# A table for the full-array work between attention visits: two linear attention layers and two segment-memory layers on one Trainium2 core

## The chip, the cores and the metric

The kernel runs on one core of one Trainium2 chip. The metric is device time in microseconds for one execution; lower is better. Before the change the median of three runs is 1875.67 us (1871.93 to 1879.55).

## The reference

The input x has 2048 tokens of 512 features in float32. Four layers follow each other, A, B, A, B, each on the layer norm of x and each added to x. The weights of the two A layers are the same, and those of the two B layers too. There are 32 heads of 16 features.

```python
# A: linear attention with a learned feature map
phi_q = concat([softmax(pq), softmax(-pq)])          # pq = q @ w_phi per head
phi_k = concat([softmax(pk), softmax(-pk)])
kv, z = phi_k^T v, sum(phi_k)
o = (phi_q kv) / (phi_q z + 1e-6);  x = x + o @ wo

# B: four segments of 512 tokens, causal softmax inside, a memory across
for s in range(4):
    logits = qs @ ks^T * scale + mask;  a_dot = softmax(logits) @ vs
    pq = elu1(qs);  a_mem = (pq M) / (pq z + 1e-6)
    o = g * a_mem + (1 - g) * a_dot                   # g = sigmoid(beta) per head
    pk = elu1(ks);  M = M + pk^T vs;  z = z + sum(pk)
x = x + o @ wo
```

Here elu1(t) is t + 1 for positive t and exp(t) otherwise.

## The kernel before, in words

**Precision and shapes.** Every large product of the projections is split into a high and a low float32r part, and three products (high-high, high-low, low-high) for each of four blocks of 128 input features are summed. So one result tile of 128 x 512 is a *group of twelve products* of 128x128 by 128x512 (`mm3`, L304). Its result stands in a PSUM tile with the tag `g`; there are three of these (`G = 3`). The attention products have tiles of their own, one each: `lg` for logits, `mx` for maxima, `pv` for values.

**Layer A** (L431) has two passes. Pass 1 takes keys and values of all tokens into one state; its queries go to DRAM. Pass 2 (L544) takes the 16 token tiles of 128 in turn: eight transposes of the features, eight products with the state KN, four transposes of the result (`turn`, L319) and one group of twelve for the output projection. A tile uses a `g` tile six times.

**Layer B** (L580) runs in steps k (L874). One *visit* is 4 heads of one segment of 512 tokens, 8 visits to a segment and 32 in all, and five steps to a visit (`R = 5`). In each step from k = 0 to 159 TensorE first multiplies logits (`attend`, L751), from which ScalarE makes the exponential P, and GpSimd masks it. From k = -9 it multiplies the logits of a later visit once more for their maxima (`maxima`, L710), which VectorE reduces to one number a row. In steps 0 and 2 of a visit the values follow (`weighted`, L787). Steps 1, 3 and 4 (`FILL`, L32) have a *gap* instead: full-array work of other parts. A visit further needs `put_maxima` (L742, one transpose and a copy back into the queries) and `finish` (L814, four transposes of the attention result U and, on VectorE, a reciprocal and a product `wt`, in `weigh`, L343).

**What fills the gaps.** For each segment: the layer norm of its tokens and their transposes (`norm_T`, L257); eight query and key projections (`proj`, L633), four values (`values`, L607) and four output projections of the segment before (`out`, L822), 16 groups of twelve; the memory's reads, transposes and update (`memory`, L658). From k = -31 to about 1 the rest of pass 2 of the layer A before runs in the same steps, from its token tile 7 on. In the last segment of the first layer B the norm and the values of the next layer A's first segment come along.

**What sets the order.** TensorE's instructions are chained in the order in which the code issues them while the steps run (`held`, L107). From k = 3 VectorE, ScalarE and GpSimd are chained likewise (`Ordered`, L89). A planner decides what stands in a gap. `plan` (L840) gives each job its slots and a cost; at each slot it issues products one by one until the job's due share is done. `rest` (L863) holds values and output projections, which are issued, also one by one, until the gap has the work that `FULL` names. So a projection is stretched over eight to ten steps, a values or output group often over several gaps, and while it is open it keeps its `g` tile. The call at the centre is:

```python
while rest and k >= rest[0][1] and (work[0] - begun + own < full[max(k - R, 0) // (8 * R)]
                                    or k >= rest[0][2]):
```

**Other steps that the change touches.** `queue_w` (L625) issues the DMA for the weights of a later projection; two weight tiles `w4` are in flight. `stack` (L699) copies the parts of a projection by six DMAs into the row layout of the attention products, at step 0 of a visit, three visits ahead of its logits. `phi` (L616) makes the feature map of a projection in the step after it: two activations on ScalarE, two operations on GpSimd. `residual` (L331) loads the tile of x to which an output projection is added. All these DMAs are issued by SyncE's queue.

Of the kernel before, what the change touches and what calls it, by code (L numbers as in the profile page):

```python
# [18 lines left out]
P = 128  # L19
NSEG = 4  # L20
# [26 lines left out]
SIDE = 1.0  # L47
# [4 lines left out]
def interleave_kernel(ctx, tc, x_in, a_wqkv, a_wphi, a_wo, b_wq, b_wk, b_wv, b_wo, b_beta,  # L52
# [251 lines left out]
    def mm3(po, lhs, rhs, fine=False):  # L304

        n = 0
        for kc in range(NC):
            for a, b in ((0, 0), (0, 1), (1, 0)):
                mm(po, lhsT=lhs(a, kc), rhs=rhs(b, kc), start=(n == 0), stop=(n == 11))
                n += 1  # L310
                if fine and n < 12:
                    yield
            if not fine:
                yield

    def tok_proj(po, hT, t, w, fine=False):
        yield from mm3(po, lambda a, kc: hT[a][:, kc, t * P : (t + 1) * P], lambda b, kc: w[b][:, kc, :], fine)
# [19 lines left out]
    def out_proj(x, xdst, i, o, w, fine=False):  # L337
        po = PS("g", G)
        yield from mm3(po, lambda a, kc: o[a][:, kc * P : (kc + 1) * P], lambda b, kc: w[b][:, kc, :], fine)
# [20 lines left out]
    def v_tile(hT, w, vv, tag, fine=False):  # L360
# [4 lines left out]
        for t in range(4):  # L365
            po = PS(*tag)
            yield from tok_proj(po, hT, t, w, fine)
            act.copy(v[:, t, 0 : H * VW].rearrange("p (h e) -> p h e", e=VW)[:, :, 0:DH],
                           po.rearrange("p (h e) -> p h e", e=DH))

# [60 lines left out]
    class LayerA:  # L431
# [4 lines left out]
        def pass1(self, first):  # L436
            hTs, vv = [], []
            norm = norm_T(self.xsrc, 0, hTs)
# [141 lines left out]
    class LayerB:  # L580
# [21 lines left out]
        def turned(self, s):  # L602

            for _ in self.ng:
                yield

        def values(self, s):  # L607
            self.vv[s] = []
            yield from v_tile(self.hT[s], self.wv, self.vv[s], ("g", G), True)
            self.valued = s  # L610
# [4 lines left out]

        def phi(self, d, m, pp):  # L616
            e = T2("tb2", TB2)
            r = T2("tb3", 2)
            act.activation(e, pp, AF.Exp)
            act.activation(r, pp, AF.Relu)  # L620
            pool.tensor_scalar(e, e, 1.0, None, op0=MIN)
            pool.tensor_tensor(out=e, in0=e, in1=r, op=ADD)
            d["phi", m] = e
# [9 lines left out]
        def proj(self, s, c):  # L633
            d = self.st[s, c] = {}
            hT = self.hT[s]
            need = (s > 0, s < NSEG - 1)
            for m in range(2):
                w = self.w4.pop(0)
                pp = PS("g", G)
                yield from mm3(pp, lambda a, kc: w[:, a, kc, :], lambda b, kc: hT[b][:, kc, :], True)  # L640
                self.queue_w()
                hi, lo = d["part", m] = [self.part() for _ in range(2)]
                act.copy(hi, pp)
                dve.tensor_tensor(out=lo, in0=pp, in1=hi.bitcast(F32), op=SUB)
# [4 lines left out]
            self.ready.add(s * NC + c)  # L649
# [8 lines left out]
        def memory(self, s, c):  # L658
# [14 lines left out]
            if s < NSEG - 1:  # L673
# [7 lines left out]
                assert self.valued >= s  # L681
# [140 lines left out]
        def out(self, s):  # L822
# [4 lines left out]
            for t in range(4):  # L827
                cur, xc = oT, x
                if t < 3:
# [3 lines left out]
                yield from out_proj(xc, self.xdst, 4 * s + t, cur, self.wo, True)  # L833
# [6 lines left out]
        def plan(self, extra):  # L840


            S = 8 * R

            def span(a, b):
                return [k for k in range(a, b) if self.filled(k)]

            yield from extra
            yield self.turned(0), span(-30, -26), 0
# [21 lines left out]
        def filled(self, k):  # L871
            return k < -LEAD or k % R in FILL
# [145 lines left out]
```

## Time and profile before

| what | value |
|---|---|
| median of three runs | 1875.67 us (1871.93 to 1879.55) |
| the profiled execution's own time | 1861.92 us |
| its span, first to last instruction | 1860.2 us |
| mean granted TensorE clock | 0.950 |
| busy: TensorE, its weight loads | 1584.2 us (85%), 1116.3 us (60%) |
| busy: VectorE, ScalarE, GpSimd | 1182.7 us (64%), 789.8 us (42%), 542.3 us (29%) |
| chain of work that ended last | TensorE 60%, VectorE 23%, ScalarE 6%, DMA 4% |

In the profile PE is TensorE, PEld its weight loads, DVE VectorE, ACT ScalarE, POOL GpSimd, SP SyncE. A row names the result tile and its inputs: `g<-w,hh` is a product of the values projection, `g<-w,oh` of an output projection, `g<-hh,wqk` of a query or key projection, `g<-ident,U` a transpose of U. L119 is the line of every product and L123 that of every transpose, since both go through a helper; L98 is the line of every instruction of the other three engines that the ordering class issues. In square brackets or behind the bar stands how long the engine was idle before an instruction, and what ended that. A group of products that waits for a buffer is put down to whoever read that buffer last. The page's times are of one execution.

### The profile page before, as it was taken

To read this page: it belongs to the slowest core of one execution; us is meant where nothing else is said; L and a number is where in the kernel's file an instruction comes from. 1 tells how busy PE (TensorE), PEld (TensorE's weight loads), DVE (VectorE), ACT (ScalarE), POOL (GpSimd) and SP (SyncE) were. 2 spreads that over 40 slices of the span, in tenths; PEclk is the share of its full clock that TensorE was granted. 3 is DMA by queue.
4 is the path that set the end of the run, shared out by engine and by line. 5 is a ranking of instruction groups with operands and counts; after the bars stand their busy time and mean duration, and the time that the engine had idled before them with its cause. 6 is when DMAs were issued, how large, how long until landed. Compare 5 with 4: busy or idle time off the path is not lost.

```text
span 1860.2 us, 28201 instructions
## 1 busy us (share of the span) xinstructions
PE 1584.2 (85%) x9856; PEld 1116.3 (60%) x9856; DVE 1182.7 (64%) x3358; ACT 789.8 (42%) x1202; POOL 542.3 (29%) x840
## 2 busy tenths in 40 slices
PE   5999897778888888897999998877888888888987
PEld 4888775544555555554568887665455555555544
DVE  4676773367777567567736676625767766665783
ACT  6443242125555345355533333311365544453543
POOL 3322320113433334232230233210234423332322
PEclk9999898899999999998999998988999999999999
DMA  9512343323444333234422035322433233333321
GB/s 317 190 55 88 92 135 136 91 75 102 126 119 116 86 78 105 81 108 148 132 94 76 23 93 169 102 85 80 131 105 95 75 100 89 92 80 83 97 68 46
DMA packets 99974, 193.68 MB, mean 104 GB/s; under 512 B 13432, under 2 KB 27000, under 8 KB 96760
## 3 DMA queue, kind: packets, MB, share of 16 engines
q1 hardware_dynamic: 98680, 191.35, 34.4%
q8 instruction: 79, 1.29, 0.3%
q10 hardware_dynamic: 1152, 0.52, 0.1%
q14 instruction: 63, 0.52, 0.1%
HBM read 96.86 MB, written 41.94 MB: 75 GB/s over the span
## 4 chain that ended last, share of the span: by engine, by line
PE 60%; DVE 23%; ACT 6%; DMA 4%; issue 4%; SPq 1%; POOL 1%; POOLq 0%; DVEq 0%; ACTq 0%
PE g L119 38%; DVE mx L98 12%; PE mx L119 7%; PE lg L119 6%; PE g L123 5%; PE pv L119 4%; ACT P L98 2%; DVE mxs L98 2%; DMA x<-x 1%; DVE es L98 1%; ACT ta L98 1%; ACT x L98 1%; DMA tb<-pq 1%; DVE ta L98 1%; DVE r L98 1%
## 5 line engine op out<-in xcount | busy, mean ns | idle before, releaser
L98 DVE CUSTOM_DVE_ANT_0 mx<-mx,mask 128x128 f32<-128x128 f32 (+3 forms) x1024 | 510.2, 498 | 238.0 <-PE mx L119 213.8
L98 ACT ACTIVATE P<-lg 128x1024 f32<-128x1024 f32 x320 | 328.1, 1025 | 319.2 <-PE lg L119 310.2
L98 POOL TENSOR_SCALAR_AFFINE_SELECT P<-P 128x256 f32<-128x256 f32 (+1 forms) x448 | 190.6, 439 | 638.8 <-ACT P L98 638.7
L119 PE MATMUL mx<-e,e 63*128 63x256 f32 (+2 forms) x1024 | 155.2, 361 | 60.0 <-DVE mxs L98 52.4
L119 PE MATMUL g<-w,oh 128*128 128x512 f32 x512 | 186.7, 442 | 15.8 <-DVE tmp L98 8.4
L119 PE MATMUL g<-w,hh 128*128 128x512 f32 x512 | 181.2, 421 | 10.4 <-DVE ot L98 5.3
L119 PE MATMUL g<-hh,wqk 128*128 128x512 f32 x512 | 184.9, 417 | 5.1 <-ACT tb L98 2.3
L119 PE MATMUL lg<-e,e 64*128 64x256 f32 (+2 forms) x1024 | 171.9, 394 | 17.0 <-ACT P L98 16.9
L119 PE MATMUL pv<-P,v 128*32 128x512 f32 (+3 forms) x2048 | 164.4, 439 | 0.1
L119 PEld LDWEIGHTS lg<-e,e 64*128 64x128 f32 x1024 | 83.7, 191 | 127.7 <-issue 68.8
L119 PEld LDWEIGHTS mx<-e,e 63*128 63x128 f32 x1024 | 85.4, 192 | 106.2 <-DVE mxs L98 89.0
L98 DVE DVE_READ_ACCUMULATOR2_ANT mxs<- 128x1 f32 x1024 | 144.6, 141 | 0.0
L98 POOL TENSOR_SCALAR tb<-tb 128x512 f32<-128x512 f32 x48 | 71.3, 1485 | 180.0 <-ACT tb L98 177.0
L119 PEld LDWEIGHTS g<-w,oh 128*128 128x128 f32 x512 | 100.1, 208 | 37.8 <-issue 10.7
L119 PEld LDWEIGHTS g<-hh,wqk 128*128 128x128 f32 x512 | 101.4, 199 | 31.5 <-ACT tb L98 3.5
L119 PEld LDWEIGHTS g<-w,hh 128*128 128x128 f32 x512 | 96.7, 195 | 34.8 <-issue 7.6
L119 PEld LDWEIGHTS pv<-P,v 128*32 128x32 f32 x2048 | 53.5, 109 | 102.0 <-issue 95.0
L119 PE MATMUL g<-w,ol 128*128 128x512 f32 x256 | 111.9, 437 | 0.0
L119 PE MATMUL g<-hl,wqk 128*128 128x512 f32 x256 | 107.0, 418 | 0.0
L98 DVE TENSOR_REDUCE es<-P 128x64 f32<-128x1024 f32 x64 | 76.6, 1196 | 44.8 <-ACT P L98 44.7
L119 PE MATMUL g<-w,hl 128*128 128x512 f32 x256 | 104.8, 409 | 0.0
L119 PE MATMUL g<-KN,P 128*128 128x68 f32 x512 | 78.8, 314 | 27.6 <-DVE ol L98 14.4
(117 smaller groups left out, 2588.1 us busy)
## 6 DMA issues: line engine op xcount, KB each, us to landing
e<-ta SPq DMA_DIRECT2D x264, 128.0 KB
wqk<-wqk SPq DMA_DIRECT2D x64, 512.0 KB
x<-x SPq DMA_DIRECT2D x48, 256.0 KB
e<-U SPq DMA_DIRECT2D x80, 128.0 KB
pq<-tb SPq DMA_DIRECT2D x32, 256.0 KB
tb<-pq SPq DMA_DIRECT2D x32, 256.0 KB
xr<-x SPq DMA_DIRECT2D x29, 256.0 KB
x<-in SPq DMA_DIRECT2D x28, 256.0 KB
```

The costliest lines, as they stand in the source:

```text
L98: i = f(*a, **k)
L119: return held(nc.tensor.matmul(*a, **k))
L123: return held(nc.tensor.transpose(*a))
```

## The change

The planner goes. A table names, for each gap of a segment, what is issued in it; `m.j` is step j of visit m, and a plus sign marks work for the next segment. `max` and `fin` are `put_maxima` and `finish`; `q`, `k`, `v` are whole groups of a query, key or values projection, `out` a whole group of the output projection; `a`, `t`, `m` are the memory's reads, transposes and update; `n`, `ln`, `load` are steps of the layer norm; `turn` is the four transposes ahead of an output projection. A second table serves the last segment, and a third, `BEFORE`, the steps from -30 to -1. In a gap the small work stands first and the group last, and no group is open when the next step begins. `proj` now issues its twelve products at once, and its feature map is split: the exponential ahead of the next step's value products, the rest behind them. Pass 2 of the layer before is spread over the steps up to k = 1 by a similar due share as before, but ahead of the named work of each step. The first norm of the second layer A gets two more pauses.

```diff
-NORM = (-1, 1, 4, 6, 8, 9, 11, 13)
-LEFT = 51700
-LAST = 2
-FULL = (1950, 2400, 2400, 1750, 0)
-LESS = 1200
-MEM0 = ((13, 16), (18, 21), (24, 26), (29, 31))
-MEM = ((-12, -11, 3, 6), (1, 4, 8, 9), (11, 13, 14, 16), (18, 19, 21, 23))
+LEFT = 53000
+GAPS = """
+0.1 max a1 k2    | 0.3 a1 fin v3   | 0.4 m0 turn
+1.1 max n q3     | 1.3 fin n out   | 1.4 n t1 turn
+2.1 max a2 n k3  | 2.3 a2 fin n out | 2.4 ln ln m1
+3.1 max ln ln turn | 3.3 fin q0+   | 3.4 t2 out
+4.1 max a3 turn k0+ | 4.3 a3 fin out | 4.4 m2
+5.1 max q1+      | 5.3 fin v0+     | 5.4 t3
+6.1 max a0+ k1+  | 6.3 a0+ fin v1+ | 6.4 m3 load
+7.1 max n q2+    | 7.3 fin n v2+   | 7.4 t0+
+"""
+LAST = """
+0.1 max a1 k2    | 0.3 a1 fin v3   | 0.4 turn
+1.1 max n q3     | 1.3 fin n out   | 1.4 n turn
+2.1 max a2 n k3  | 2.3 a2 fin n out | 2.4 n
+3.1 max n turn   | 3.3 fin ln ln   | 3.4 out
+4.1 max a3 ln ln turn | 4.3 a3 fin out | 4.4
+5.1 max v        | 5.3 fin v       | 5.4
+6.1 max v        | 6.3 fin v       | 6.4
+7.1 max n        | 7.3 fin         | 7.4
+"""
+BEFORE = {-30: "ln0", -29: "ln0", -28: "ln0", -27: "ln0", -25: "q0", -23: "v0", -21: "k0", -19: "v1", -17: "v2",
+          -14: "q1", -12: "v3", -10: "k1", -5: "load", -4: "max n q2", -2: "n", -1: "t0"}
...
-            norm = norm_T(self.xsrc, 0, hTs)
+            norm = norm_T(self.xsrc, 0, hTs, slow=not first)
...
-        def proj(self, s, c):
...
-            for m in range(2):
-                w = self.w4.pop(0)
-                pp = PS("g", G)
-                yield from mm3(pp, lambda a, kc: w[:, a, kc, :], lambda b, kc: hT[b][:, kc, :], True)
-                self.queue_w()
...
-                if need[m]:
-                    self.later.append(lambda m=m, pp=pp: self.phi(d, m, pp))
-                if m == 0:
-                    yield PAUSE
+        def proj(self, s, c, m):
+            d, hT, w = self.st.setdefault((s, c), {}), self.hT[s], self.w4.pop(0)
+            pp = PS("g", G)
+            for _ in mm3(pp, lambda a, kc: w[:, a, kc, :], lambda b, kc: hT[b][:, kc, :]):
+                pass
+            self.queue_w()
+            hi, lo = d["part", m] = [self.part() for _ in range(2)]
+            act.copy(hi, pp)
+            dve.tensor_tensor(out=lo, in0=pp, in1=hi.bitcast(F32), op=SUB)
+            if not (s == 0 if m == 0 else s == NSEG - 1):
...
+                def first():
+                    act.activation(e, pp, AF.Exp)
+                def second():
+                    act.activation(r, pp, AF.Relu)
+                    pool.tensor_scalar(e, e, 1.0, None, op0=MIN)
+                    pool.tensor_tensor(out=e, in0=e, in1=r, op=ADD)
+                self.later += [first, second]
...
-                yield from out_proj(xc, self.xdst, 4 * s + t, cur, self.wo, True)
+                for _ in out_proj(xc, self.xdst, 4 * s + t, cur, self.wo):
+                    pass
+                yield
...
+            slots = [k for k in range(BEGIN, 2) if k < -LEAD or k % R in FILL]
+            for k in range(BEGIN, R * N + 4):
...
+                later, self.later = self.later, []
+                for f in later[:1]:
+                    f()
                 if k % R in (0, 2) and 0 <= k // R - 1 < N:
                     self.weighted(k // R - 1, k % R == 2)
...
+                for f in later[1:]:
+                    f()
+                if k in slots:
+                    want = LEFT * (1 + slots.index(k)) / len(slots) if k < slots[-1] else 1e9
+                    while spent + 100 < want:
+                        before = work[0]
+                        if next(side, None) is PAUSE:
+                            break
+                        spent += work[0] - before
+                what, s = table.get(k, ((), 0))
+                for w in what:
+                    do(w, s, k)
+                if 18 <= k < 28 and k % R in FILL:
+                    next(weights, None)
```

More of the change, by code (lines that the diff above doesn't have):

```diff
@@ L310, in mm3, with tok_proj @@
                 n += 1
[L311 to L317, printed above, removed]
+            yield
+    def tok_proj(po, hT, t, w):
+        yield from mm3(po, lambda a, kc: hT[a][:, kc, t * P : (t + 1) * P], lambda b, kc: w[b][:, kc, :])
     def turn(ot):
@@ L942, in steps @@
-                now = [job for job in jobs if job[1][0] <= k]
-                proj = [job for job in now if job[0].__name__ == "proj"]
-                for job in now:
-                    if job not in proj:
-                        go(job, k)
-                own = sum(max(due(job, k)[0] - job[3], 0) for job in proj)
-                while rest and k >= rest[0][1] and (work[0] - begun + own < full[max(k - R, 0) // (8 * R)]
-                                                    or k >= rest[0][2]):
-                    if next(rest[0][0], rest) is rest:
-                        rest.pop(0)
```

168 lines of the change are left out of this document (66 added, 102 removed).

## The prediction

> **What bounds the kernel now.** I read the busy shares first (TensorE 85% of the span, VectorE 64%), then busy time by stage, what TensorE waits for in the middle segments, and the timeline of single visits. Counting TensorE's instructions in program order against the trace dates every step: layer B starts its steps (k = -31) at 265.2 us and 1178.7 us, the maxima (k = -9) at 365.0 and 1276.5, segment 0 at 402.4 and 1313.5, segment 1 at 524.6 and 1435.8, segment 2 at 672.3 and 1583.2, segment 3 at 823.6 and 1734.8, the last attention step at 940.0 and 1836.4.
>
> Busy time by stage (columns: length; busy us of TensorE, its weight loads, VectorE, ScalarE, GpSimd; granted clock; DMA share):
>
> ```profile
> 265.00:365.00 100.00, 76.77 (x363) 60.97 (x362) 41.90 (x83) 25.45 (x42) 13.25 (x12) 0.85 0.35 115
> 365.00:402.00 37.00, 26.30 (x130) 18.12 (x130) 20.76 (x71) 4.87 (x9) 2.76 (x2) 0.95 0.23 67
> 402.00:525.00 123.00, 104.48 (x742) 63.97 (x741) 90.36 (x309) 67.99 (x98) 44.08 (x78) 0.99 0.43 124
> 525.00:672.00 147.00, 125.57 (x856) 79.72 (x852) 98.64 (x334) 70.67 (x102) 54.15 (x89) 0.95 0.34 92
> 672.00:823.00 151.00, 126.22 (x856) 79.22 (x855) 98.50 (x334) 69.04 (x98) 49.45 (x86) 0.95 0.34 93
> ...
> 1735.00:1837.00 102.00, 87.28 (x662) 48.68 (x666) 70.75 (x242) 53.02 (x68) 33.81 (x67) 1.00 0.26 70
> ```
>
> TensorE is 77% busy in the first stage and 85% in segments 1 and 2, at a granted clock of 0.85 and 0.95. What it waited for in those two segments:
>
> ```profile
> PE g L119 <- DVE wt L98: 13.9, 6, 2.3
> PE mx L119 <- DVE mxs L98: 8.5, 15, 0.7
> PE g L123 <- DVE wt L98: 4.6, 2, 2.3
> PE g L123 <- DVE ot L98: 3.7, 2, 2.2
> ```
>
> The wt wait, eight times 2.3 us, comes in step 3 of a visit, right behind the four transposes of `finish`:
>
> ```profile
> 742.38 0.65 PE L123 MATMUL g<-ident,U 128*128 128x128 f32 x4
> 742.49 0.30 DVE L98 CUSTOM_DVE_ANT_0 mx<-mx,mask 128x128 f32<-128x128 f32 x1 [0.66 <-PE mx L119]
> ...
> 744.42 0.25 DVE L98 RECIPROCAL r<-g 128x16 f32<-128x16 f32 x1
> 744.77 0.42 DVE L98 TENSOR_TENSOR wt<-g,r 128x256 f32<-128x256 f32 x1
> 745.28 0.72 POOL L98 TENSOR_TENSOR ot<-ot,wt 128x256 f32<-128x256 f32 x1 [1.33 <-DVE wt L98]
> 745.32 0.53 PEld L119 LDWEIGHTS g<-mem,tb 128*128 128x128 f32 x4 [2.52 <-issue]
> 745.35 0.70 PE L119 MATMUL g<-mem,tb 128*128 128x136 f32 x4 [2.31 <-DVE wt L98]
> 745.80 0.97 PE L119 MATMUL g<-w,oh 128*128 128x512 f32 x2
> ```
>
> The mem product does not read wt. It waits for a buffer: there are three g tiles, one is held by an open projection, one by an open values or output group, and the third by the transposes of U, which VectorE reads only after the maxima of this step (742.49 to 744.56). Where nothing but the open group follows the transposes (817.62 and 818.03 us) they cost 0.41 us, not 2.97. After the wait a product takes 0.43 us (746.56 to 746.99) instead of 0.23, for some microseconds.
>
> **The change, part by part.** The work is the same; only its place changes. Durations are the timeline's, start to start: a product 128x512 0.23 us, so a group of twelve 12 x 0.23 + 0.2 for entering and leaving = 2.96; four transposes 0.41 to 0.45; logits 0.50 with two tile widths or one of 512, 0.34 when a step reaches them unmixed; maxima products 0.49 or 0.33; a value step 1.21; two mem products 0.47. On VectorE the maxima of a step allow the next maxima products, from start to start, no sooner than 2.05 us (two of 512 columns), 2.7 (128 and 384) or 2.65 (four of 256). The thinly filled visit from 1807.3 us takes 12.6 us, near these five.
>
> *Open groups gone, fin wait gone.* In the built program each g tile of the new kernel takes the buffer of a tile whose last product lies six or more TensorE instructions back, and mostly twenty or more; in the old one several take that of the tile just before. So I take the buffer waits as 0. Bounds: 0, and the 2.3 us of now, if VectorE is still late.
>
> *Uneven gaps, a new wait.* Gaps 1 and 3 get a whole group, gap 4 mostly 0.4 to 1.4 us of small work. There the maxima of four 256 columns are not covered: from maxima products to maxima products 2.65 us, of which TensorE has 0.33 + 0.41 + 0.34. That is a stall of 1.6 us in nearly every visit. Next late behind it are, on VectorE, the four maxima and the logits' exponential on ScalarE (1.03 us, done before).
>
> *Evacuation at gap 1.* A projection's copy (ScalarE 0.59) and subtraction (VectorE 0.69) stand ahead of the next maxima; today that costs 0.55 us at step 1 (logits to maxima 1.05 instead of 0.50, in most visits), then at step 3. Same price, moved.
>
> A visit with groups in gaps 1 and 3 is then 0.50 + 0.49 + 0.11 + 2.96 (step 1), 1.94 (step 2), 0.50 + 0.50 + 0.49 + 0.41 + 2.96 (step 3), 0.34 + 2.65 (step 4), 0.33 + 1.21 (step 0) = 15.4 us; with two memory reads 16.3; with a `turn` in gap 4 its subtraction delays the next maxima by 0.55. Visits 2 and 3 carry the norm. There `n` at 2.1 puts the norm's VectorE chain and two 0.82 us ScalarE activations ahead of the projection's copy: about 1.8 us more (now the same chain costs 2.0 us, at 438.5 us). Segments 1 and 2: 16.9 + 16.0 + 19.4 + 16.7 + 16.8 + 15.4 + 16.3 + 15.4 = 133 us each, against 147.7 and 151.3 (second layer 147.4 and 151.6).
>
> Segment 0 has few groups; visits are bound by the maxima at 14 to 15.4 us, 122 in all by the same terms, against 122.2 and 122.3. Segment 3: 115.5 against 116.4 in the first layer; in the second, whole groups sit in gaps that were evenly filled, so visits 0 to 4 take 16.9 + 16.0 + 16.3 + 13.5 + 14.6 = 77.3 (now 72.5), visit 5 takes 12.2 and the last two 16.5 as now: 106.0 against 101.6.
>
> *Pass 2 beside the projections, k = -31 to -9.* Now a projection and a values group are open nearly all the time, and the six g tiles of a pass-2 token tile go through one buffer: 99.8 us for seven token tiles and some 70 other products. Alone, a tile takes 6.1 us (233.38 to 239.48 to 245.57). After: 7 x 6.1 + 8 groups x 2.96 + 4 norm transposes of 0.45 = 68, plus 3 for the starts: 71. Bounds: 68, and 99.8. From -9 to 0 nine steps, bound by the maxima or by their products, add to 2.7 + 2.1 + 2.7 + 4.6 + 2.1 + 5.1 + 2.6 + 2.7 + 3.1 + 2 for the weighing that shares VectorE = 30, against 37.4 (second layer 97.8 and 37.0).
>
> *Moves costed at nothing.* Weight loads for the next projection are issued at the group's end, two visits ahead of use; the norm's x loads go from 7.4 to 6.4, the wo pieces from steps 28 to 34 to steps 18 to 26, residual loads with their turns. All pass SP's queue at about 0.6 us each, some nine in a 15 us visit; were that cover gone, a stack landing late would hold the maxima, 0.6 us for each DMA ahead of it. No DMA appears among the waits of the short visits of segment 0. The feature map's second half (ScalarE 0.60, GpSimd 1.49 + 1.28) goes behind the value products: GpSimd's masks queue behind it, but have a visit to spare. The slow first norm of the second layer A only adds yields.
>
> **Sum.** First layer: 28.8 + 7.4 + 0.2 + 14.7 + 18.3 + 0.9 = 70.3 us saved. Second: 26.8 + 7.0 + 0.3 + 14.4 + 18.6 - 4.4 = 62.7. Together 133.0 off the profiled execution's 1861.9 us (span 1860.2) = 1728.9. That execution lies 0.74% under the median of the runs, 1875.67; scaled the same, 1742 us.
>
> **Rivals.**
> *Slower: VectorE at gap 4.* It is 65% busy in segments 1 and 2 (98.6 of 151), and the same work in 133 us is 74%. If what stands ahead of the maxima there (mem add 0.34, turn 0.68, hl 0.69 each) stretched the 2.65 us, every visit would pay. It decides from 133 over 56 filled visits = 2.4 us a visit; at 3 us it gives 1729 + 168 = 1897, scaled 1911. Against: the two largest such pieces together are 1.4 us and occur in two visits of eight.
> *Part of it.* Pass 2 stays bound by its own chain of copies and weighing and saves half (1729 + 35, 1777 scaled), or each filled visit loses another 0.6 us to VectorE's order (1763, 1776).
> *No change.* The 2.3 us is VectorE's lateness and not a buffer: it would be met again at gap 3's group, 1876. Against: 818.03 above.
> *The clock.* In the first stage the grant is 0.85 and products run at half pace after waits. If 1.6 us of idling in each visit brought segments 1 and 2 there, some 115 us of TensorE work in each of the four stretches stretch by 0.95/0.85: 4 x 13.5 = 54 us, 1796 scaled. Against: 1735 to 1837 us waits for maxima or exponentials in nearly every visit and reads 1.00. [...]
> *More.* Smaller stalls at gap 4 and a full clock give 1742 - 30 = 1712.
>
> **How the numbers follow.** Forecast (1725 to 1760) 0.47, part of it 0.25, more 0.14, clock 0.04, no change 0.03, slower 0.07. From 1705 to 1808 holds the forecast, nearly all of "part" and "clock" and two thirds of "more": a little over 0.8. About 0.5% is what a measurement of this kernel tells from no change. Faster 0.90, same 0.03, slower 0.07.
>
> **What would show it.** After the transposes of U, a next product 0.41 us on; no wt among TensorE's long waits; k = -31 to 0 near 100 us; segments 1 and 2 near 133; instead, 1.6 us of waiting for mxs at step 0 of most visits, so that wait's total rises well above 52.4 us; the grant above 0.95 in the first stage. It is wrong if mxs waits grow beyond 4 us a visit, or if pass 2 still spaces its token tiles by 14 us or more.

## The result, and the profile after

The changed kernel takes 1781.51 us, the median of four runs (1776.08 to 1788.87), beside 1877.61 us for the kernel before on the same chip. The ratio is 0.9485, with a 95% interval from 0.943 to 0.954. Forecast were 1742 us, with a range from 1705 to 1808. So the direction and the range held, and the size did not: 96 us were saved by the medians, 133 were forecast.

The profiled execution of the new kernel took 1788.87 us (span 1787.2), 73.1 us less than the profiled one of before. It stands 0.4% above its median, as the old one stood 0.7% under its own. The two profiles therefore understate the difference, and the 60 us that are missing against the forecast of 1728.9 are partly this. The table dates the steps as in the prediction, in us.

| stretch, steps k | before, layer 1 / 2 | forecast | after, layer 1 / 2 |
|---|---|---|---|
| -31 to -9 | 99.8 / 97.8 | 71 | 83.7 / 77.8 |
| -9 to 0 | 37.3 / 37.0 | 30 | 30.9 / 32.8 |
| segment 0 | 122.2 / 122.3 | 122 | 128.8 / 124.0 |
| segment 1 | 147.7 / 147.4 | 133 | 132.8 / 133.0 |
| segment 2 | 151.3 / 151.6 | 133 | 134.3 / 135.7 |
| segment 3 | 116.3 / 101.6 | 115.5 / 106 | 122.9 / 116.8 |
| last step to last product | layer 2: 20.0 | unchanged | layer 2: 25.5 |

Busy time by stage of the kernel after (columns as before: length; busy us of TensorE, its weight loads, VectorE, ScalarE, GpSimd; granted clock; DMA share; GB/s). The first five rows are the first layer's. The last row is segment 3 of the second layer.

```profile
263.00:347.00 84.00, 76.14 (x398) 63.95 (x397) 43.99 (x87) 26.81 (x45) 13.19 (x12) 0.89 0.46 144
347.00:378.00 31.00, 23.26 (x116) 16.74 (x112) 20.56 (x70) 4.90 (x10) 2.75 (x2) 0.89 0.24 77
378.00:506.00 128.00, 108.14 (x723) 66.44 (x719) 89.87 (x305) 66.53 (x98) 45.83 (x79) 0.91 0.42 116
506.00:639.00 133.00, 120.52 (x857) 78.19 (x856) 97.97 (x335) 69.62 (x103) 54.09 (x89) 0.99 0.39 102
639.00:773.00 134.00, 121.34 (x852) 78.44 (x852) 96.03 (x330) 67.43 (x99) 49.47 (x86) 0.97 0.39 104
...
1641.00:1758.00 117.00, 98.44 (x661) 55.18 (x665) 71.84 (x247) 50.92 (x65) 31.48 (x65) 0.85 0.23 60
```

TensorE is now about 90% busy in segments 1 and 2, at a grant of 0.96 to 0.99 over both layers where it was 0.95 to 0.96. In the last row the grant went the other way, from 1.00 to 0.85.

The timeline of visit 1 in segment 2, step 3 to step 0 (columns: start, length, engine, line, operation, in brackets the idle time before and what ended it):

```profile
665.82 0.65 PE L141 MATMUL g<-ident,U 128*128 128x128 f32 x4
...
666.23 0.70 PE L137 MATMUL g<-w,oh 128*128 128x512 f32 x2
...
667.86 0.25 DVE L116 RECIPROCAL r<-g 128x16 f32<-128x16 f32 x1
...
668.21 0.42 DVE L116 TENSOR_TENSOR wt<-g,r 128x256 f32<-128x256 f32 x1
...
669.17 0.50 PE L137 MATMUL lg<-e,e 64*128 64x256 f32 x4
...
672.07 0.51 PE L137 MATMUL mx<-e,e 63*128 63x512 f32 x2 [0.71 <-DVE st L116]
```

The output group starts 0.41 us behind the transposes of U. VectorE still reads them only at 667.86, as late as before, but nobody waits for it: the group has a tile of its own. The new wait stands at 672.07, where the maxima of the next step are not covered. What TensorE waited for in segments 1 and 2 of the first layer (us in total, times, longest):

```profile
PE mx L137 <- DVE mxs L116: 15.9, 30, 0.9
PE lg L137 <- ACT P L116: 4.9, 7, 1.4
```

No wait for wt or ot is left there. In the whole trace the wait for maxima rose from 52.4 to 83.0 us, and that for P from 16.9 to 33.9. That these had been hidden behind the waits removed is likely, but no run shows it by itself.

### The profile page after: what moved, and what is told of

Read it like the earlier page. It is cut to its first block, busy times and chain, and to the rows that moved or that the text cites. A ratio compares the mean times of both kernels' runs of the same rounds, so it can differ in the third digit from the quotient of the medians.

```text
span 1787.2 us, 28142 instructions
## 1 busy us (share of the span) xinstructions
PE 1573.1 (88%) x9856; PEld 1121.8 (63%) x9856; DVE 1178.3 (66%) x3358; ACT 782.1 (44%) x1202; POOL 543.6 (30%) x840
## 4 chain that ended last, share of the span: by engine, by line
PE 60%; DVE 24%; ACT 5%; DMA 5%; issue 3%; SPq 1%; POOL 0%; POOLq 0%; ACTq 0%; DVEq 0%
PE g L137 39%; DVE mx L116 13%; PE mx L137 8%; PE lg L137 5%; PE pv L137 5%; PE g L141 4%; DVE mxs L116 2%; ACT P L116 1%; DMA x<-x 1%; DMA tb<-pq 1%; DMA e<-ta 1%; ACT ta L116 1%; ACT x L116 1%; DVE ta L116 1%; DVE mmq L116 1%
## 5 line engine op out<-in xcount | busy, mean ns | idle before, releaser
L137 PE MATMUL mx<-e,e 63*128 63x256 f32 (+2 forms) x1024 | 163.2, 377 | 103.3 <-DVE mxs L116 83.0
L137 PE MATMUL lg<-e,e 64*128 64x256 f32 (+2 forms) x1024 | 175.7, 401 | 36.2 <-ACT P L116 33.9
L137 PEld LDWEIGHTS mx<-e,e 63*128 63x128 f32 x1024 | 89.9, 198 | 159.6 <-DVE mxs L116 118.6
L137 PE MATMUL g<-w,oh 128*128 128x512 f32 x512 | 181.6, 438 | 6.6 <-ACT oh L116 5.4
L137 PE MATMUL pv<-P,v 128*32 128x512 f32 (+3 forms) x2048 | 180.9, 475 | 0.1
L137 PE MATMUL g<-hh,wqk 128*128 128x512 f32 x512 | 178.6, 410 | 0.0
L137 PEld LDWEIGHTS lg<-e,e 64*128 64x128 f32 x1024 | 84.5, 192 | 135.7 <-ACT P L116 74.4
L137 PE MATMUL g<-w,hh 128*128 128x512 f32 x512 | 165.3, 403 | 0.5 <-DVE e L116 0.5
L137 PEld LDWEIGHTS g<-hh,wqk 128*128 128x128 f32 x512 | 99.0, 193 | 20.9 <-issue 0.6
L137 PEld LDWEIGHTS g<-w,hh 128*128 128x128 f32 x512 | 94.1, 191 | 18.7 <-DVE e L116 0.7
L137 PE MATMUL g<-hl,wqk 128*128 128x512 f32 x256 | 101.6, 397 | 0.0
L137 PE MATMUL g<-w,hl 128*128 128x512 f32 x256 | 100.8, 394 | 0.0
L137 PE MATMUL g<-w,e 128*128 128x512 f32 x384 | 97.7, 396 | 0.0
```

The costliest lines, as they stand in the source:

```text
L137: return held(nc.tensor.matmul(*a, **k))
```

## The experiments

All dates of steps are made as in the table above. Stretches whose code is unchanged differ by some us from run to run: segment 2 of the second layer took 132.9 to 135.7 us in four kernels that have it in common. Where only a single execution was made, that is said.

### Whole groups under the old planner

Theory: the open groups' buffers cost the time. Rival: the places that the table names do.

```diff
 # v_tile of the kernel before; out and proj likewise
-            yield from tok_proj(po, hT, t, w, fine)
+            for _ in tok_proj(po, hT, t, w):
+                if not fine:
+                    yield
...
+            if fine:
+                yield
 # go
-                while job[3] + 100 < want if cost else job[3] < n:
+                while job[3] + (2600 if cost in (5450, 10900) else 100) < want if cost else job[3] < n:
```

> The kernel before with one thing of the change alone: its planner still chooses the gaps from costs and due times, but a projection, a values tile and an output tile each issue their twelve products at once (a projection when its budget reaches a whole group, so that it ends about where the open one ended). No group is open across a visit, and nothing is named by a table. If the open groups' buffers cost the time, the waits of TensorE for wt (29.4 and 10.2 us in all) go, segments 1 and 2 come to 135 to 140 us each (before 147.7 and 151.3) and the steps -31 to 0 to 110 to 120 us in each layer (before 137 and 135): in all 70 to 95 us off, 1780 to 1805 us. If the places named in the table bring the gain, segments 1 and 2 stay above 145 us and the time above 1850 us.

Measured: 1779.42 us (1768.47 to 1781.55), ratio 0.9462 (0.9414 to 0.951). This small edit alone gives what the whole change gives. Segments 1 and 2 take 135.4, 136.8, 135.8 and 136.9 us, and wt is not among the waits of TensorE that come to 2.7 us or more. Its busy time by stage, for -31 to -9, segment 1 and segment 2 of the first layer:

```profile
265.00:330.00 65.00, 60.77 (x352) 50.49 (x353) 40.00 (x82) 25.46 (x42) 13.35 (x12) 0.97 0.52 168
...
499.00:634.00 135.00, 119.40 (x856) 76.88 (x854) 98.32 (x334) 70.12 (x102) 54.08 (x89) 1.00 0.37 100
634.00:771.00 137.00, 121.56 (x858) 78.25 (x856) 98.16 (x334) 68.49 (x98) 49.29 (x86) 0.99 0.41 118
```

The first stretch is 65 us here and 84 in the kernel after, though both have whole groups. Some of that is work that stands later: 36 fewer products, 8.3 us. Over -31 to 40 together the sums are 233.8 and 231.6 us, against 243.4 and 234.6 in the kernel after and 259.3 and 257.1 before. So the table gains 1 to 3 us in each of segments 1 and 2, and loses 3 to 10 us a layer ahead of them and 3 to 6 in segment 3.

### One tile and two tiles held open

Theory: any tile held open across a visit costs its neighbours their buffers. This puts such tiles back into the new kernel, without moving anything else.

```diff
+            def hold(n, tiles):
+                def half(pg, first):
+                    mm(pg, lhsT=self.wv[0][:, 0, 0:P], rhs=self.wv[0][:, 0, :], start=first, stop=not first)
+                for pg in tiles:
+                    half(pg, False)
+                tiles[:] = [PS("g", G) for _ in range(n)]
+                for pg in tiles:
+                    half(pg, True)
...
+                if 8 * R <= k <= 24 * R + 1 and k % R == 1:
+                    hold(1 if k < 24 * R else 0, open_)   # the other kernel: 2
```

> The kernel after, with one g tile held open all through segments 1 and 2: a product of 128x512 opens it in gap 1 of a visit, a second one closes it in gap 1 of the next, and the next is opened there; its sums are read by nobody. That is 2 x 0.23 = 0.46 us of work a visit, 3.7 us a segment. If tiles held open cost time by the buffers that they take, two free tiles are nearly enough: segments 1 and 2 at 137 to 145 us (after: 133 and 134). If they cost nothing, 137.

> As hold1 with two tiles held open at a time, as in the kernel before when a projection and a values or output group were both unfinished: 4 x 0.23 = 0.92 us of work a visit, 7.4 us a segment. By the buffers each g tile now waits for the reader of the one just before it: the wait of 2.3 us behind the transposes of U is back in each visit, wt stands again among what TensorE waits for, and segments 1 and 2 take 133 + 7.4 + 18 = 158 us or more. If open tiles cost nothing, 140 to 142 us.

Measured, in single executions: 1870.94 and 2064.29 us. The four segments took 152.2, 153.9, 152.2 and 153.0 us with one tile held; without the added products that is 148.5 to 150.2, about the length that they had before the change. With two tiles they took 204.0 to 204.8. Beyond the 3.7 and 7.4 us of added products that is 15 and 63 us a segment (after, mean of the four: 134.0). Segments 0 and 3, where nothing is held, stay near those of the kernel after. With one tile held TensorE does not wait for wt, but ahead of other `g` products (the two segments of the first layer):

```profile
PE g L137 <- DVE ot L116: 12.8, 7, 1.9
PE g L137 <- DVE tmp L116: 3.9, 2, 1.9
```

With the waits for hl (3.4 and 2.5 us) and tb (2.7) these come to 25.3 us, of the 31.6 us by which the two segments are longer than in the kernel after, beyond the added products. The timeline with two tiles held, at the same step of another visit:

```profile
855.10 0.66 PE L141 MATMUL g<-ident,U 128*128 128x128 f32 x4
...
857.14 0.25 DVE L116 RECIPROCAL r<-g 128x16 f32<-128x16 f32 x1
...
857.49 0.42 DVE L116 TENSOR_TENSOR wt<-g,r 128x256 f32<-128x256 f32 x1
...
858.06 1.19 PE L137 MATMUL g<-w,hh 128*128 128x512 f32 x2 [2.31 <-DVE wt L116]
...
859.05 0.63 PE L137 MATMUL g<-w,hl 128*128 128x512 f32 x1
859.48 1.05 PE L137 MATMUL g<-w,hh 128*128 128x512 f32 x2
```

This is the wait of the kernel before, 2.31 us for wt, brought back by nothing but tiles held open. Neither kernel is a copy of the one before: one held tile gives its segment length by other waits, two give its wait and segments some 48 us longer than its own. Both expected lengths were too low. With two held, other small pieces in a gap wait for a reader too, not what follows the transposes of U alone; in the two segments of the first layer TensorE waited for wt, ot, hl and tb:

```profile
PE g L137 <- DVE wt L116: 20.6, 13, 2.3
PE g L141 <- DVE ot L116: 15.3, 7, 2.4
...
PE g L141 <- DVE hl L116: 9.7, 6, 2.1
PE g L141 <- ACT tb L116: 8.8, 4, 2.6
```

### Small work behind the group

The change also says that small work stands ahead of the group. Here that alone is reversed.

```diff
+                big = [w for w in what if w.rstrip("+0123456789") in ("q", "k", "v", "out")]
+                if k >= 0:
+                    what = big + [w for w in what if w not in big]
```

> The kernel after with the order inside each gap from step 0 on reversed: the whole group of twelve first, the small work (transposes of maxima and of U, memory, norm, turns) behind it. No group is held open. If what costs time is a tile held over other work, nothing is held here either and it stays within 10 us of 1781. If small work ahead of the group matters by itself, because VectorE's and ScalarE's part of the small work then stands right ahead of the next step's maxima and exponentials with no products to cover it, two such gaps a visit lose 0.5 to 1 us each: segments 1 and 2 at 141 to 149 us in place of 133, and 1830 us or more.

Measured: 1837.53 us (1835.06 to 1841.17), ratio 0.9794 (0.9748 to 0.984); segments 1 and 2 at 141.8, 141.0, 142.0 and 139.9 us. So the order inside a gap is worth 56 us by itself, with no group open. The wait for P rises from 33.9 to 57.9 us and that for maxima from 83.0 to 94.0. The visit shown above reads here (TensorE's timeline):

```profile
688.62 0.49 PE L137 MATMUL lg<-e,e 64*128 64x512 f32 x2
690.81 0.50 PE L137 MATMUL mx<-e,e 63*128 63x512 f32 x2 [1.70 <-DVE st L116]
```

The wait at the maxima is 1.70 us instead of 0.71. VectorE's rows of the same step say why:

```profile
687.20 0.25 DVE L116 RECIPROCAL r<-g 128x16 f32<-128x16 f32 x1
687.55 0.42 DVE L116 TENSOR_TENSOR wt<-g,r 128x256 f32<-128x256 f32 x1
687.89 0.69 DVE L116 BATCH_NORM_STATS2 bs<-x 128x6 f32<-128x512 f32 x1
...
688.71 0.41 DVE L116 CUSTOM_DVE_ANT_0 mx<-mx,mask 128x256 f32<-128x256 f32 x1
```

The weighing of U and the norm's statistics, which in the kernel after are worked off while the group runs, now stand behind it and ahead of the maxima. TensorE had issued the products for these at 687.26; the first of them is reduced 1.45 us later (in the kernel after 0.44 us, 669.51 to 669.95).

### The table ahead of segment 0

```diff
-BEFORE = {-30: "ln0", -29: "ln0", -28: "ln0", -27: "ln0", -25: "q0", -23: "v0", -21: "k0", -19: "v1", -17: "v2",
-          -14: "q1", -12: "v3", -10: "k1", -5: "load", -4: "max n q2", -2: "n", -1: "t0"}
+BEFORE = {-30: "ln0", -29: "ln0", -28: "ln0", -27: "ln0", -21: "q0", -20: "v0", -16: "k0", -14: "v1",
+          -11: "q1", -7: "v2", -6: "k1", -5: "load", -4: "max n q2", -2: "n v3", -1: "t0"}
```

> The kernel after with another table of the steps ahead of segment 0 alone: q0 -21, v0 -20, k0 -16, v1 -14, q1 -11, v2 -7, k1 -6, v3 -2 in place of q0 -25, v0 -23, k0 -21, v1 -19, v2 -17, q1 -14, v3 -12, k1 -10, which is about where the kernel before with whole groups has them. Pass 2 keeps its steps. If a group's copies and feature map on ScalarE, ahead of pass 2's copies, are what made the steps -31 to -9 longer than forecast, those steps fall from 83.7 and 77.8 to 62 to 67 us with fewer products in them (some 8 us of that are two or three groups that now stand later), and the steps -31 to 40 together fall by 5 to 10 us in each layer: 1762 to 1772 us. If the places there do not matter, the sum stays within 2 us of 243.4 and 234.6, and the time at 1781.

Measured: 1762.32 us (1759.54 to 1766.73), ratio 0.9383 (0.9308 to 0.9458). The steps -31 to 40 fall from 243.4 to 232.0 us and from 234.6 to 229.8. How the kernel after lost them shows in its timeline around k = -20, right behind the projection k0:

```profile
298.24 0.42 DVE L116 TENSOR_TENSOR tmp<-g,r 128x256 f32<-128x256 f32 x1
...
303.30 1.04 PE L141 MATMUL g<-ident,P 128*128 128x128 f32 x8
...
303.50 0.59 ACT L116 CAST ta<-g 128x512 fp32r<-128x512 f32 x1 [5.81 <-PE g L137]
...
304.85 1.08 ACT L116 ACTIVATE tb<-g 128x512 f32<-128x512 f32 x2 [0.76 <-DVE ta L116]
...
305.98 0.65 PE L141 MATMUL g<-ident,tmp 128*128 128x128 f32 x4 [1.65 <-ACT tb L116]
...
307.21 1.08 ACT L116 COPY P<-g 128x512 f32<-128x512 f32 x2
...
308.19 3.03 PE L137 MATMUL g<-KN,P 128*128 128x68 f32 x16 [1.55 <-DVE ol L116]
...
311.96 0.63 PE L137 MATMUL g<-w,ol 128*128 128x512 f32 x1
...
312.39 1.05 PE L137 MATMUL g<-w,hh 128*128 128x512 f32 x2
```

k0's copy and its two feature map activations stand on ScalarE ahead of pass 2's copies of P, so TensorE waits twice, 1.65 and 1.55 us, with no group left to fill it. The first is again a wait for a `g` tile. The transposes at 305.98 read tmp, which VectorE had finished at 298.66, and not tb. But k0's result and the two results of P's transposes take all three tiles, and the wait ends with the feature map (tb), the last reader of k0's. (The rows leave buffer numbers out, so this is read from what ended the wait.) Behind these waits a product takes 0.43 us from start to start instead of 0.23 (311.96 to 312.39). In the busy time by stage of the kernel with the other table, the stretch from -31 to -9 reads:

```profile
266.00:334.00 68.00, 61.77 (x362) 51.87 (x361) 42.35 (x86) 25.27 (x42) 13.55 (x12) 0.97 0.50 165
```

The grant is 0.97 where it was 0.89. From -31 to -9, dated to a tenth, TensorE is busy for 61.4 of 67.6 us here and for 75.8 of 83.7 us in the kernel after. Of the 14.5 us between the busy times the 36 products that stand later are 8.3; the other 6 are pace. Idle time differs by 1.6 us only. In the second layer, at grants of 0.94 and 0.96, busy time falls by 7.2 us and idle time by 2.0.

### Groups split over gaps 3 and 4

```diff
 # v_tile, and out likewise: a pause after six products
-                if not fine:
+                if not fine or n == 1:
 # steps: values 0 to 2 and outputs in gap 3 finish at the end of gap 4
+                    if k % R == 3 and k > 0 and i < 3:
+                        half.append(val[s])
...
+                if half and k % R == 4:
+                    next(half.pop())
```

> The kernel after, where 18 groups of a layer that stand in gap 3 (the values tiles 0 to 2 and the output tiles in gap 3) issue six products there and six at the end of gap 4. If the step behind gap 4 waits for VectorE's maxima with nothing to cover them (1.22 us at its maxima products), each such visit gets 1.2 to 1.45 us shorter: 36 visits, 43 to 52 us off, 1730 to 1740 us. If VectorE sets the length of the whole visit, the wait only moves to another step: within 8 us of 1781. If one tile held open from gap 3 to gap 4 is enough to bring the buffer waits back, waits for wt show again and the time is above 1790 us.

Measured: 1750.75 us (1748.02 to 1759.7), ratio 0.9337 (0.9286 to 0.9388). The direction is as expected, the size is not: 31 us instead of 43 to 52. TensorE's timeline in the visit shown above:

```profile
659.30 0.66 PE L141 MATMUL g<-ident,tb 128*128 128x128 f32 x4
659.71 0.70 PE L137 MATMUL g<-w,oh 128*128 128x512 f32 x2
...
661.72 0.50 PE L137 MATMUL lg<-e,e 64*128 64x512 f32 x2
662.20 0.50 PE L137 MATMUL mx<-e,e 63*128 63x512 f32 x2
```

The 0.71 us of waiting is gone. But that is all there was: from the logits of step 3 to those of step 1 the visit falls from 10.1 us (4.83 + 1.69 + 3.61) to 9.5 (3.47 + 3.19 + 2.88). The 1.22 us that I had read as a wait are from start to start and hold the logits' own 0.50. Segments 1 and 2 come to 129.5 to 129.9 us. A tile held for one step only brought no wait for wt back. It did bring another one, in visit 2, where gap 4 holds eight transposes of the norm and behind them the memory's update:

```profile
552.43 1.20 PE L137 MATMUL g<-v,tb 128*128 128x136 f32 x8 [1.67 <-DVE hl L116]
```

The product reads v and tb; hl is what VectorE makes as the last reader of the norm's transposes. This wait, 1.67 to 1.69 us, stands in segments 1 and 2 of both layers and nowhere in those of the kernel after, and in segment 1 of the first layer visit 2 rises from 21.9 to 23.2 us. So the split saves less in that visit than the expectation had it.

### Dummy products in the empty gaps

```diff
+                if k % R in (1, 3) and (0 <= k < 8 * R or 24 * R <= k < 32 * R):
+                    ops = {w.rstrip("+0123456789") for w in what}
+                    if not (ops & {"q", "k"} or "v" in ops and (s < NSEG - 1 or k < 25 * R or after0)
+                            or "out" in ops and s > 0):
+                        dummy(4, (self.wv if s < NSEG - 1 else self.wo)[0])
```

> The kernel after with four more products of 128x512 in each gap 1 and 3 of segments 0 and 3 that holds no group, 24 gaps in all; their sums are read by nobody. At full pace they are 24 x 4 x 0.23 = 22 us of work. If TensorE is slow in those segments because it idles too often (grant 0.85 to 0.93, value steps 2.29 us in place of 1.21), the added work gives the pace back: segment 0 from 128.8 to about 122 us, segment 3 of the second layer from 116.8 to 106 to 110, grant above 0.95, and the whole 10 to 20 us shorter, about 1765. If the half pace is only in time that TensorE would have waited for VectorE anyway, those segments stay within 2 us each or grow by up to 6 us each, 1781 to 1800 us.

Measured: 1771.55 us (1768.8 to 1775.27), ratio 0.9433 (0.9393 to 0.9473), which overlaps that of the kernel after. (`after0` is true in the first layer.) Inside, the parts differ. Segment 3 of the second layer is 110.6 us, with nine times four products more than in the kernel after. That had 116.8 there, and five other kernels with the same code in this segment 112.5 to 117.0, at grants of 0.92 to 0.87. Here the busy time by stage reads:

```profile
1635.00:1745.00 110.00, 97.42 (x693) 57.04 (x691) 71.40 (x245) 50.74 (x64) 31.21 (x66) 0.95 0.24 63
```

At step 147 of the second layer the sixteen value products, which had no dummies beside them, fall from 2.29 us to 1.21. In segment 0 the dummies gain 1 to 4 us (125.7 and 121.2, against 127.0 to 128.8 and 124.0 to 125.0 in four kernels with the same code), and in segment 3 of the first layer they cost 1 to 4 (126.3 against 122.5 to 125.7). So in the last segment the half pace is lost time that added work gives back: 2 to 6 us by one profiled execution of each kernel. The runs as a whole don't show the 10 to 20 us expected.

### The end of a layer

```diff
-        def out(self, s):
+        def out(self, s, early=False):
...
+                if early and t < 3:
+                    oT = turn([o[:, t + 1] for o in ot])
```

> The kernel after, where the last four output tiles (behind the last visit) turn tile t+1 ahead of the products of tile t, as the kernel before did. If the order of turn and products explains the longer end, the time from the last attention step to the end goes from 25.5 back to about 20 us in each layer, and nothing else moves: 8 to 11 us off in all, about 1772. If the products' half pace explains it, the end stays within 2 us of 25.5.

Measured, in a single execution: 1770.59 us. From the last attention step to the last product the second layer takes 19.2 us instead of 25.5 (before 20.0), which the order of turn and products explains. Behind the first layer the stretch up to the next layer B takes 3.4 us less, 238.3 instead of 241.7; in five other kernels with the same code there it took 239.4 to 245.0, so this difference is not clear of the spread.

### The norm in visit 2

Visits 2 and 3 of a segment were forecast at 19.4 and 16.7 us; in segment 1 they took 21.9 and 16.9.

```diff
-2.1 max a2 n k3  | 2.3 a2 fin n out | 2.4 ln ln m1
+2.1 max a2 k3 n  | 2.3 a2 fin n out | 2.4 ln ln m1
```

> The kernel after with the order of two things in gap 2.1 exchanged: the projection k3 ahead of n, so that the norm's chain on VectorE and its two activations stand behind the projection's copy and subtraction. If that order is what made visits 2 and 3 longer (22.0 us where 19.4 was forecast), they lose 1.5 to 3 us in segments 0 to 2 of both layers, 9 to 18 us in all, about 1768. If VectorE's whole load of that visit sets its length, it stays within 0.7 us and the time at 1781.

Measured, in a single execution: 1784.95 us; visit 2 takes 22.5 us in segments 1 and 2 of the first layer, 20.9 and 23.9 in the second. So my reason, that the norm's chain stands ahead of the projection's copy, falls. The timeline of the kernel after shows another:

```profile
679.62 0.56 PE L137 MATMUL lg<-e,e 64*128 64x256 f32 x4
...
680.08 1.52 ACT L116 ACTIVATE x<-x,st 128x512 f32<-128x512 f32 x2 [3.29 <-DVE st L116]
...
681.97 1.02 ACT L116 ACTIVATE P<-lg 128x1024 f32<-128x1024 f32 x1
...
683.04 0.30 PEld L137 LDWEIGHTS lg<-e,e 64*128 64x128 f32 x4 [1.90 <-ACT P L116]
```

The norm's two activations, 1.52 us, sit between the logits of step 2 and their exponential P, and they do so wherever the projection's copy stands: the next logits wait for P for 1.40 us in the kernel after and 2.81 us in this one. The last run below moves them.

### The edits together

The first kernel joins the split, the other table and the order at the end; the second adds dummy products in the last segment of the second layer; the third adds this:

```diff
-2.1 max a2 n k3  | 2.3 a2 fin n out | 2.4 ln ln m1
-3.1 max ln ln turn | 3.3 fin q0+   | 3.4 t2 out
+2.1 max n a2 k3  | 2.3 n a2 fin out | 2.4 n m1
+3.1 max ln ln turn | 3.3 ln ln fin q0+   | 3.4 t2 out
 # norm_T, of layer B's later segments: a pause between the chain and the first activation
+        if slow == 2:
+            yield
```

> Three edits on the kernel after, together: the 18 groups of a layer split over gaps 3 and 4 (1750.75 alone against 1781.5), the other table ahead of segment 0 (1762.3 alone), and turn t+1 ahead of the products of tile t at the end (3 and 6 us of the two ends alone). They lie in different stretches, so they should add: 31 + 16 + 9 = 56 us off, 1725 us, 1720 to 1732. If a part of each gain was only a better grant in that run, less is left: 1735 to 1750.

> As combo, with four products of 128x512, read by nobody, in the gaps 1 and 3 of visits 2 to 7 of the second layer's segment 3 (from step 131 on) that hold no projection or output group. If idling too often slows TensorE there, that stretch falls from the 107.5 us that the split alone gave by 2 to 5 us, and the whole to 1722. If the split has already taken the long waits away, the dummies cost up to 5 us: 1725 to 1730.

> The kernel combo with the norm of the next segment spread differently: its VectorE chain in gap 2.1 ahead of the memory product, its first two ScalarE activations (1.52 us together) in gap 2.3 and the other two in 2.4, its transposes in 3.1 and 3.3. In gap 2.1 those activations stand between the logits of step 2 and their exponential. If that is what makes visit 2 long (22 to 23.5 us in the kernels after and combo), the value step there falls from 2.7 to 1.2 us, the products behind it run at 0.23 us each, and visits 2 and 3 together lose 2 to 4 us in segments 0 to 2: 12 to 24 us off, 1705 to 1716 us. If the same work only waits elsewhere, as when the projection was put ahead of the norm, the two visits keep their sum within 1 us and the time stays at 1728.

Measured:

| kernel | median, us | ratio to before | 95% interval |
|---|---|---|---|
| three edits | 1728.33 (1719.74 to 1732.98) | 0.9207 | 0.9169 to 0.9246 |
| and dummy products | 1727.43 (1716.11 to 1730.08) | 0.9191 | 0.9146 to 0.9235 |
| three edits and the norm | 1716.35 (1708.96 to 1723.98) | 0.9126 | 0.9096 to 0.9157 |

The three edits add, as expected: 53 us off the kernel after. The dummies change nothing that these runs can tell, though their stretch read 103.7 us in place of 107.1. In segments 1 and 2 of the three edits alone visit 2 took 23.0, 23.4, 21.9 and 26.2 us, now 17.0, 18.7, 17.1 and 17.1; visit 3 went from 16.1 to 19, since the transposes moved there. ScalarE's timeline at the same step reads now:

```profile
665.42 0.59 ACT L116 CAST U<-g 128x512 fp32r<-128x512 f32 x1 [4.55 <-PE g L137]
665.99 1.03 ACT L116 ACTIVATE P<-lg 128x1024 f32<-128x1024 f32 x1
```

P follows the projection's copy at once. The norm's activations were one cause, but not the only one. In segment 1 of the first layer, step 2 of the visit falls from 3.43 to 1.93 us: its wait of 1.43 us for P is gone. Step 4 falls from 5.96 to 3.17 us: with the transposes moved out of gap 4, the wait of 1.68 us behind them is gone too, the one that the split had brought. Step 3 falls from 5.69 to 3.97 us. The run moves activations and transposes together and so does not divide what lies beyond these two waits.

This kernel is the fastest of the study, 3.7% under the changed kernel by the medians.

## Why the prediction was right or wrong

**The wait at finish: right.** The prediction put the 2.3 us to the buffers of open groups, and named 817.62 us of the old trace, where nothing but the open group follows, as the evidence. In that place the old trace reads:

```profile
817.62 0.66 PE L123 MATMUL g<-ident,U 128*128 128x128 f32 x4
818.03 0.71 PE L119 MATMUL g<-w,hh 128*128 128x512 f32 x2
```

Whole groups alone took the waits for wt away, one held tile brought back the old length of the segments by waits for other readers, two the old wait of 2.31 us for wt. The rival "no change", in which VectorE's lateness would be met again, is out: VectorE reads U as late as before (2.04 us behind the transposes' start, at 665.82 and 667.86), and TensorE has gone on. The held tiles show the price of a shorter rotation here, 15 us a segment with two tiles left and 63 with one.

**Segments 1 and 2: right in the sum, by terms that cancel.** 133 us each were forecast, 132.8 to 135.7 measured. Visit by visit (segment 1, layer 1) the forecast was 16.9, 16.0, 19.4, 16.7, 16.8, 15.4, 16.3, 15.4, and the trace has 16.8, 14.8, 21.9, 16.9, 15.8, 15.2, 16.4, 15.1. The stall behind gap 4 was mis-sized: 1.6 us of idling in nearly every visit were forecast, and the 30 waits for maxima in these sixteen visits add to 15.9 us, 1.0 a visit. That excess paid for visit 2, where the term "about 1.8 us more" failed in its mechanism too: not the order of the norm and the projection's copy, but two activations ahead of the exponential, 1.4 us of waiting in step 2. The rest of what visit 2 lost is not divided by any run.

**Pass 2 beside the projections: the largest miss in one stretch, 12.7 and 6.8 us.** The step that failed is "68, plus 3 for the starts". It counted TensorE's work as if pass 2's own chain were covered, and left out that a projection's copy and feature map are three ScalarE instructions (1.67 us) that stand ahead of pass 2's copies. "So I take the buffer waits as 0" failed here too: that went by how far back the last product of a tile lies, but k0's tile is taken until its feature map has read it, and this cost 1.65 us at 305.98. TensorE is idle for 7.9 and 7.7 us of the stretch in the two layers. And the pace was not whole: the same products keep it busy for 75.8 us in the first layer and 70.2 in the second, at grants of 0.89 and 0.96. The part "pass 2 stays bound by its own chain of copies" of the second rival named the waits on that chain, but not what lengthens them. The other table, with no other change, came to 67.5 and 68.6 us; that stretch holds 36 products fewer, so the 71 us were not reached with the forecast's work either.

**The clock: the right mechanism at the wrong place.** The rival expected segments 1 and 2 at 0.85. They ran at 0.96 to 0.99, although they idle at a maxima product in most visits. The loss came beside pass 2 in the first layer (0.89) and, above all, where groups are few: segment 0 at 0.91, segment 3 of the second layer at 0.85, where the old kernel, with its products spread evenly, had 0.99 and 1.00. The prediction used just that 1.00 as evidence against the rival, and overlooked that the change itself takes the even filling away there. It missed 6.8 and 2.0 us in segment 0, and 7.4 and 10.8 us in segment 3. The dummies show that in segment 0 (grants of 0.93 and 0.99 with them, 0.91 and 0.93 without) and in the last segment (0.95 and 0.85) the pace was a part of this, 1 to 6 us each; in segment 3 of the first layer they leave it open. Products ran at 0.43 us instead of 0.23 behind single waits of 2.31 us (745.35 us in the kernel before, 858.06 with two tiles held), and behind two of 1.65 and 1.55 us (305.98 and 308.19 us in the kernel after).

**The end: a step that was not priced.** The sum took the end as unchanged, though the diff moves `turn` behind the group of the tile before. That cost 5.5 us in the second layer, and undoing it gave 6.3 back.

**The slower rival.** VectorE's order was to decide from 2.4 us a visit. It did not come near in the kernel after, since the table has small work ahead of the group; with the order reversed the price was 7.2 us a segment, 0.9 a visit. What the prediction did not see is how much of the gain hangs on this order. The places that the table names bring none of it in all, as the old planner's places with whole groups show (1779.42 us).

**What would show it.** Of the signs named, the 0.41 us, the missing wt, segments near 133 and the higher wait for maxima came. The grant above 0.95 in the first stage (0.89) and 100 us for -31 to 0 (114.6 and 110.6) did not. By the medians the forecast missed by 39.5 us, by the profiles by 60; the 20 between them are the place of the two profiled executions among their runs. By stretch, the misses in the table add to 59.5 us: 27.0 in segments 0 and 3, 23.2 ahead of segment 0, 5.5 at the end and 3.8 in segments 1 and 2.

## What to carry to other kernels

A PSUM tile that stays open over other work was paid for here by whoever shares its pool, with 15 us a segment for one of three and 63 for two: if a short wait is put down to the reader of a tile that the waiting product does not read, count the tiles and close the groups before moving any work. Count a tile as taken until its last reader is done, not its last product (k0's cost 1.65 us). Closing every group is not the aim in itself: here a tile held over one step cost a wait of 1.7 us in one visit of a segment and still left 31 us of gain. Then put, inside each gap, first what other engines have to finish and last the products that cover it (56 us here), and look on every engine's queue for what stands between a step and the instruction that the next step waits for (two activations ahead of P cost 1.4 us). Where a stretch has little work left, spread it: TensorE's grant in the last segment fell from 1.00 to 0.85, as that in the full segments 1 and 2 rose from 0.95 or 0.96 to between 0.96 and 0.99.

## What was not expected of the hardware

With 36 products of 128x512 added, the last segment was 2 to 6 us shorter in one profiled execution, with the grant at 0.95 instead of 0.85 to 0.92. In the kernel after TensorE idled twice between 304 and 309 us, for 1.65 and 1.55 us; the grant read 0.99 there and 0.50 from 309 to 313. In the kernel before it was 0.54 from 746.0 to 747.2 us, behind a single wait of 2.31 us. In segments 1 and 2 of the kernel after, waits for maxima of up to 0.9 us in most visits went with grants of 0.96 to 0.99. One tile of three held open cost a segment 15 us here and two cost 63, four times as much for twice the tiles.
